# Tying the matmuls of the first pass to the written order of two layers, and gathering the token sums in half of each expert

## The chip, the cores and the metric

One core of a Trainium2 chip runs the whole program. The metric is the device time of one execution in microseconds (us), given as a median over several executions.

## The reference

The model is a causal attention whose output feeds a mixture of eight experts. Only the second half matters here:

```python
x = attention(q, k, v, s)            # 2304 tokens x 512
P = sinkhorn(exp(x @ w_gate))        # 2304 x 8, eight rounds of normalizing
out = 0
for e in range(8):                   # each expert: 512 -> 1024 -> 512
    h = maximum(x @ w1[e], 0)
    out += P[:, e:e+1] * (h @ w2[e])
```

All of it is float32. The kernel gets that precision from a matmul type with fewer mantissa bits by splitting each operand into a high and a low part and adding three products (high x high, high x low, low x high).

## The kernel before

Expert 0 is done beside the attention. The other seven experts are done in three passes of 768 tokens. A pass is 28 units (7 experts of 4 units); a unit is 256 of an expert's 1024 hidden columns.

**Layer 1** of a unit is a 2x2 block product with seven block products instead of eight (a scheme of the Strassen family). `SEQ` gives the order of these seven ops: 11, T3 (of the unit before), T1, T4 (of the unit before), 22, 21, T2. `step1` issues one op: six matmuls of 384 columns (line 959) into one of three PSUM buffers named `c` (Z, A and B of the unit). Between two ops that use the same buffer, ScalarE copies (`t`) or VectorE adds (`z`, line 253) read it, and `relu_split` turns the sum into the two parts of a hidden tile `h`: a ScalarE relu (line 923) and after it a VectorE instruction (line 924). The hidden tiles lie in 18 buffers, four to a unit. One link is closer than the others: op 21 takes the buffer that op T4 of the unit before leaves, once the relu and the VectorE instruction have read it, and only op 22 stands between them.

**Layer 2** of the first pass is plain. `step2p(idx, i, ui, ci)` issues one block: six matmuls of 512 columns (line 1077) into a PSUM buffer `zz`, for expert `idx`, half `i` of its tokens, unit `ui` and token chunk `ci`. An expert has 24 blocks: 12 with `i` = 0, then 12 with `i` = 1. The pass has 168 blocks, and 196 ops of layer 1.

**The first pass** begins with 26 ops of layer 1. Then `plain_item` writes layer 2 block by block, and before each block as many ops of layer 1 as `pace` (28 ops in 24 blocks) allows: one, and at every sixth block two (T4 and 22).

**What else runs beside it.** `prep_w2` splits the raw `w2` of a unit (tile `r`) into `w2p`: a ScalarE cast (line 110), a GpSimd subtraction (line 111). Then it asks SyncE for the raw `w2` two units on. `sum_w2` makes sums of `w2` for the later passes on VectorE (tile `sb`, lines 250 and 253 are the helpers that issue each add and subtraction) and stores them (`w2d`). `w1_ahead` makes sums of `w1` (tile `s`) on VectorE and splits `w1` (`wp`) on ScalarE and GpSimd. `x_sums`, the generator `side`, makes token sums for the third pass in 43 small pieces on VectorE (tiles `sx`, `sc`, `sh`) with loads and stores. `behind()` ties instructions behind the latest `relu_split` on their engine, as far as the written order had got.

**Who sets the order.** The text of the kernel gives each instruction its priority. A planner that simulates the engines then orders each engine's instructions: at each moment the instruction of highest priority whose inputs it takes to be ready. So the two layers need not run in the written order. `tc.issue_after(m)` forces an instruction behind `m` on the same engine, without a semaphore. On the chip each engine takes its instructions in the planner's order.

Of the kernel before, what the change touches and what calls it, by code (L numbers as in the profile page):

```python
# [8 lines left out]
F32 = mybir.dt.float32  # L9
F32R = mybir.dt.float32r  # L10
AF = mybir.ActivationFunctionType
ALU = mybir.AluOpType
AX = mybir.AxisListType

P = 128
B, H, S, D = 4, 8, 576, 64
NT, DM, E, F = B * S, H * D, 8, 1024
# [3 lines left out]
NFC = FU // P  # L21
UPE = F // FU
# [23 lines left out]
def fused_kernel(ctx: ExitStack, tc: tile.TileContext, qT, kT, v, s, w_gate, wu, out):  # L46
    nc = tc.nc
# [57 lines left out]
    acc = {}  # L105
    cur = {}

    def split(dst, lo, src):

        nc.scalar.copy(dst, src)  # L110
        nc.gpsimd.tensor_tensor(out=lo, in0=src, in1=dst.bitcast(F32), op=ALU.subtract)

    def split_piece(u, pc, raw):
        if pc % 2 == 0:
# [212 lines left out]
    def load_head(h):  # L327
# [23 lines left out]
        out=s_sb, in0=s_sb, scalar1=0.0, scalar2=8.0, op0=ALU.max, op1=ALU.mult  # L351
# [12 lines left out]
        out=mask,  # L364
# [299 lines left out]
    for ti in range(NS + 3):  # L664
        if ti < NS:
            g, i = slots[ti]
# [154 lines left out]
    LEAD1 = 5  # L821
# [3 lines left out]
    def load_w1(si):  # L825
        if si < len(steps1):
            n, o, _ = steps1[si]
            t = hp[1].tile([P, 2, 2, P], F32R, name="w1o", tag="w1o", bufs=LEAD1 + 1)
            w1s[n, o] = t
            nc.sync.dma_start(  # L830
                out=t.rearrange("p a k c -> p a (k c)").bitcast(F32),
                in_=w1d[unit(n)][:, WOPS.index(o)],
            )
# [76 lines left out]
        hops[n, o] = t  # L910
        return t

    mark = {}

    def behind():
        st = ExitStack()
        for m in mark.values():
            st.enter_context(tc.issue_after(m.ins))
        return st

# [18 lines left out]
    def step1(si):  # L939
        n, o, q = steps1[si]  # L940
        if si >= NS1P:
            load_w1(si + LEAD1)
        else:
            w1_ahead(n if SEQ[q or 0][1] == 0 else n + 1, q)
        w = w1s.pop((n, o))
        p = items[n // UPE][0]
        x = xo[XOF[o]]
        s_ = un.setdefault(n, {})
        if o == "11":
            s_["Z"] = ps1.tile([P, 512], F32, name="c", tag="c")[:, :TP]  # L950
        if o == "T1":
            s_["A"] = ps1.tile([P, 512], F32, name="c", tag="c")[:, :TP]
        if o == "21":
            s_["B"] = ps1.tile([P, 512], F32, name="c", tag="c")[:, :TP]
        ps = s_[{"11": "Z", "T2": "Z", "T3": "Z", "T4": "Z", "T1": "A", "22": "A", "21": "B"}[o]]
        fresh = o in ("11", "T1", "21")
        for k in range(2):
            for t, (wl, xl) in enumerate(((0, 0), (0, 1), (1, 0))):
                nc.tensor.matmul(  # L959
                    ps,  # L960
                    lhsT=w[:, wl, k],
                    rhs=x[:, xl, k],
                    start=(fresh and k == 0 and t == 0),
                    stop=(k == 1 and t == 2),
                    skip_group_check=True,
                )
        if o == "11":
            s_["t1"] = tmp("t", 4)
            nc.scalar.copy(s_["t1"], ps)
        elif o == "T1":  # L970
            s_["t5"] = tmp("t", 4)
            nc.scalar.copy(s_["t5"], ps)
        elif o == "22":
            s_["t53"] = tmp("t", 4)
            nc.scalar.copy(s_["t53"], ps)
        elif o == "21":
            s_["z11"] = tmp("z", 4)
            add(s_["z11"], ps, s_["t1"], nc.vector)
            relu_split(n, "11", s_["z11"])
        elif o == "T2":  # L980
            s_["z12"] = tmp("z", 4)
            add(s_["z12"], ps, s_["t53"], nc.vector)
            relu_split(n, "12", s_["z12"])
        elif o == "T3":
            s_["z22"] = tmp("z", 4)
            add(s_["z22"], ps, s_["t5"], nc.vector)
            relu_split(n, "22", s_["z22"])
        elif n < NUP:
            relu_split(n, "21", ps)
            un.pop(n)  # L990
        else:
            c21, s1, s3, s2, s4 = (
                hp[1].tile([P, TP], F32, name="s", tag="s", bufs=5) for _ in range(5)
            )
            nc.scalar.activation(c21, ps, AF.Relu)  # L995
            clip_op(s1, s_["z22"], c21, ALU.add)
            plain_split(n, "S1", s1, nc.gpsimd)
            clip_op(s2, s_["z11"], s1, ALU.subtract)
            plain_split(n, "S2", s2, nc.vector)
            clip_op(s3, s_["z11"], c21, ALU.subtract)  # L1000
            plain_split(n, "S3", s3, nc.gpsimd)
            clip_op(s4, s_["z12"], s2, ALU.add)
            plain_split(n, "S4", s4, nc.vector)
            un.pop(n)
        if n % (UPE * (E - 1)) == UPE * (E - 1) - 1 and p + 1 < NTP:
            load_x(p + 1, XOF[o])
# [8 lines left out]
                out=r2[m].rearrange("p f d -> p (f d)"), in_=wu[unit(m), :, 1024:2048]  # L1015
            )

    def prep_w2(m):

        if m >= NUP:  # L1020
            return
        r = r2.pop(m)
        for f in range(NFC):
            w = hp[2].tile([P, 2, DM], F32R, name="w2p", tag="w2p", bufs=8)
            split(w[:, 0], w[:, 1], r[:, f])
            w2p[m, f] = w
        r2[m, "raw"] = r
        load_r2(m + 2)

    def sum_w2(m):  # L1030

        if m >= NUP:
            return
        r = r2.pop((m, "raw"))
        e, ui = divmod(unit(m), UPE)
        t13 = hp[3].tile([P, 2, DH], F32, name="sb", tag="sb", bufs=3)
        t24 = hp[3].tile([P, 2, DH], F32, name="sb", tag="sb", bufs=3)
        sub(t13, r[:, :, DH:], r[:, 0, :].rearrange("p (j d) -> p j d", d=DH), nc.vector)
        sub(t24[:, 0], t13[:, 0], r[:, 1, DH:], nc.vector)
        add(t24[:, 1], t24[:, 0], r[:, 1, :DH], nc.vector)  # L1040
        for o, t in ((0, t13), (2, t24)):
            nc.sync.dma_start(
                out=w2d[e][o : o + 2, :, ui, :].rearrange("t p d -> p t d"), in_=t
            )
# [22 lines left out]
    def step2p(idx, i, ui, ci):  # L1067
        p, e = items[idx]
        m = idx * UPE + ui
        if ui == 0:  # L1070
            zb[ci] = ps2.tile([P, 512], F32, name="zz", tag="zz", bufs=3)
        if e == 1 and ui == 1:
            scale_acc(6 * p + 3 * i + ci)
        for f in range(NFC):
            h, w = hops[m, f"{i + 1}{f + 1}"], w2p[m, f]
            for t, (a, b_) in enumerate(((0, 0), (0, 1), (1, 0))):
                nc.tensor.matmul(  # L1077
                    zb[ci],
                    lhsT=h[:, a, ci * P : (ci + 1) * P],
                    rhs=w[:, b_],  # L1080
                    start=(ui == 0 and f == 0 and t == 0),
                    stop=(ui == UPE - 1 and f == NFC - 1 and t == 2),
                )
        if ui == UPE - 1:
            c = 6 * p + 3 * i + ci
            gated(c, e, accs[c], zb[ci])
            if e == E - 1:
                store_out(c)
# [95 lines left out]
    def run1(upto):  # L1184
        nonlocal si
        while si < min(upto, len(steps1)):
            step1(si)
            si += 1
# [9 lines left out]

    xbuf = lambda a: hp[3].tile([P, 4, 2, 128], F32, name="sx", tag="sx", bufs=2)
    side = x_sums(hp[3], 2, 128, nc.vector, xbuf, nc.scalar.copy)  # L1200
    nl2 = [0]
    last = E - 2
    pace = float(si)

    def plain_item(idx):
        nonlocal pace
        for i in range(2):
            for ui in range(UPE):
                ahead = (
                    UPE * idx + 3 if (i, ui) == (0, 0)  # L1210
                    else UPE * (idx + 1) + ui - 1 if i == 1 and ui
                    else None
                )
                if ahead is not None and ahead != NUP - 1:
                    prep_w2(ahead)
                for ci in range(3):
                    if ci == 2 and ahead is not None and ahead != NUP - 1:
                        with behind():
                            sum_w2(ahead)
                    if idx < last:  # L1220
                        pace += 28 / 24
                        run1(min(int(pace), NS1P))
                        nl2[0] += 1
                        if nl2[0] > 12 and nl2[0] % 5 in (2, 4):
                            with behind():
                                next(side, None)
                    step2p(idx, i, ui, ci)

    for idx in range(last):
        plain_item(idx)  # L1230
    run1(NS1P)
    prep_w2(NUP - 1)
    sum_w2(NUP - 1)
    for _ in side:
        pass
    p0bctx.close()
    p0ctx.close()
    hp[1] = ctx.enter_context(tc.tile_pool(name="p12", bufs=1, reuse_waits="tile"))
    for k in range(LEAD1):
        load_w1(NS1P + k)  # L1240
    plain_item(last)
    p0ctx2.close()
    hp[0] = ctx.enter_context(
        tc.tile_pool(name="h12", bufs=1, side="right", reuse_waits="tile")
# [60 lines left out]
```

## Time and profile before

| what | value |
|---|---|
| median of 3 runs | 1757.98 us (1755.74 to 1759.18) |
| the profiled execution | 1764.02 us, of which the span of instructions is 1762.2 us |
| TensorE matmul busy | 1694.1 us (96%) |
| VectorE, ScalarE, GpSimd busy | 71%, 47%, 49% |
| mean granted TensorE clock | 0.987 |
| first pass, from its first op to its last block | about 436 to 907 us of the span |

PE is TensorE's matmuls, PEld its weight loads, DVE is VectorE, ACT ScalarE, POOL GpSimd, SP SyncE, which issues the transfers. The busy times overlap, so none of them alone says what limits the kernel. Row times are microseconds from the start of the span.

### The profile page before, as it was taken

How to read it: one execution, taken by the hardware profiler on the slowest of the kernel's cores; microseconds unless marked ns; L12 is line 12 of the kernel's file. 1: busy time of each engine (PE TensorE's matmuls, PEld its weight loads, DVE VectorE, ACT ScalarE, POOL GpSimd, SP SyncE). 2: the span in 40 equal slices, each digit the busy share in tenths (PEclk: the TensorE clock that was granted, in tenths of full speed). 3: DMA queues.
4: the chain of work that ended last, by engine and by line, in shares of the span. 5: the costliest groups of instructions: out<-in, count | busy, mean ns of one | idle time of the engine just before them, and what ended most of it. 6: DMA issues, size and time to landing. Idle time of an engine off the chain costs nothing.

```text
span 1762.2 us, 31207 instructions
## 1 busy us (share of the span) xinstructions
PE 1694.1 (96%) x11109; PEld 1585.5 (90%) x11109; DVE 1242.6 (71%) x2352; ACT 831.2 (47%) x1817; POOL 856.8 (49%) x761
## 2 busy tenths in 40 slices
PE   5889999999999999999999999999999999999998
PEld 4678888889888888888889999999999999999998
DVE  6867667555666767666448877777777777777775
ACT  4876665733444343433335444444444544444442
POOL 5549647512554544444414444445445554444454
PEclk9899999999999999999999999999999999999999
DMA  6667656364667658557596655565687655655652
GB/s 173 189 187 227 204 162 203 98 256 168 206 233 264 210 203 278 178 204 265 196 307 192 193 183 182 179 186 180 184 306 226 206 184 187 184 182 176 189 180 84
DMA packets 204986, 352.09 MB, mean 200 GB/s; under 512 B 21088, under 2 KB 103008, under 8 KB 204800
## 3 DMA queue, kind: packets, MB, share of 16 engines
q1 hardware_dynamic: 204512, 349.52, 62.2%
q8 instruction: 88, 1.44, 0.3%
q10 hardware_dynamic: 320, 0.59, 0.1%
q14 instruction: 66, 0.54, 0.1%
HBM read 249.94 MB, written 94.81 MB: 196 GB/s over the span
## 4 chain that ended last, share of the span: by engine, by line
PE 76%; DVE 12%; DMA 5%; issue 3%; SPq 1%; ACT 1%; POOL 1%; DVEq 0%; POOLq 0%; ACTq 0%
PE c L959 28%; PE zz L1130 12%; PE zz L1077 11%; PE y L1130 8%; PE g L146 4%; PE g L175 4%; DVE s L935 3%; PE sc L454 3%; PE pv L556 2%; PE tr L526 2%; DVE h L250 2%; PE c L146 2%; PE c L175 2%; DVE z L253 1%; DVE a L1061 1%
## 5 line engine op out<-in xcount | busy, mean ns | idle before, releaser
L250 POOL TENSOR_TENSOR w2o<-r,w2o 128x512 fp32r<-128x512 f32 x196 | 279.7, 1448 | 381.8 <-ACT w2o L1111 336.3
L1130 PE MATMUL zz<-w2o,h 128*128 128x256 f32 x2016 | 280.6, 282 | 1.4 <-DMA w1o<-w1d 1.4
L959 PE MATMUL c<-xS,w1o 128*128 128x384 f32 x1344 | 277.8, 339 | 1.6 <-DVE z L253 1.5
L1130 PEld LDWEIGHTS zz<-w2o,h 128*128 128x128 f32 x2016 | 269.6, 188 | 1.9 <-ACT h L923 1.8
L1077 PE MATMUL zz<-w2p,h 128*128 128x512 f32 x1008 | 251.8, 396 | 0.4 <-ACT h L923 0.4
L935 DVE SCALAR_TENSOR_TENSOR s<-z,s 128x384 f32<-128x384 f32 x224 | 206.4, 959 | 48.6 <-ACT s L995 43.6
L923 ACT ACTIVATE h<-z 128x384 fp32r<-128x384 f32 x252 | 130.4, 525 | 220.4 <-DVE z L253 218.6
L924 DVE SCALAR_TENSOR_TENSOR h<-z,h 128x384 fp32r<-128x384 f32 x252 | 182.5, 732 | 72.1 <-ACT h L923 68.1
L959 PEld LDWEIGHTS c<-xS,w1o 128*128 128x128 f32 x1344 | 226.4, 188 | 5.1 <-DVE z L253 2.5
L1077 PEld LDWEIGHTS zz<-w2p,h 128*128 128x128 f32 x1008 | 190.4, 190 | 35.3 <-ACT h L923 0.7
L1130 PE MATMUL y<-w2o,h 128*128 128x256 f32 x1512 | 206.4, 283 | 3.6 <-DVE a L1061 2.9
L1130 PEld LDWEIGHTS y<-w2o,h 128*128 128x128 f32 x1512 | 196.6, 188 | 8.3 <-DVE a L1061 7.2
L959 PE MATMUL c<-x,w1o 128*128 128x384 f32 x1008 | 202.4, 336 | 0.0
L253 DVE TENSOR_TENSOR z<-c,t 128x384 f32<-128x384 f32 x252 | 135.2, 549 | 70.1 <-PE c L959 69.0
L250 POOL TENSOR_TENSOR h<-s,h 128x384 fp32r<-128x384 f32 x112 | 137.9, 1237 | 85.7 <-ACT h L931 84.8
L959 PEld LDWEIGHTS c<-x,w1o 128*128 128x128 f32 x1008 | 171.2, 188 | 0.1
L1061 DVE SCALAR_TENSOR_TENSOR a<-zz,prob,a 128x256 f32<-128x256 f32 (+1 forms) x210 | 110.7, 530 | 77.1 <-PE zz L1130 52.8
L931 ACT CAST h<-s 128x384 fp32r<-128x384 f32 x224 | 112.7, 513 | 93.6 <-DVE s L935 92.4
L959 PE MATMUL c<-xS,wp 128*128 128x384 f32 x672 | 137.6, 348 | 14.8 <-DVE z L253 14.2
L959 PEld LDWEIGHTS c<-xS,wp 128*128 128x128 f32 x672 | 124.2, 196 | 21.5 <-DVE z L253 15.4
L250 POOL TENSOR_TENSOR wp<-s,wp 128x512 fp32r<-128x512 f32 x56 | 78.5, 1402 | 118.0 <-ACT wp L859 85.0
L1111 ACT CAST w2o<-r 128x1024 fp32r<-128x1024 f32 x98 | 102.5, 1047 | 58.8 <-PE y L1130 48.8
(141 smaller groups left out, 2765.1 us busy)
## 6 DMA issues: line engine op xcount, KB each, us to landing
w1o<-w1d SPq DMA_DIRECT2D x392, 256.0 KB
w1d<-wp SPq DMA_DIRECT2D x84, 512.0 KB
r<-wu SPq DMA_DIRECT2D x70, 512.0 KB
r<-w2d SPq DMA_DIRECT2D x56, 512.0 KB
sa<-wu SPq DMA_DIRECT2D x28, 512.0 KB
w2d<-sb SPq DMA_DIRECT2D x56, 256.0 KB
wraw<-wu SPq DMA_DIRECT2D x22, 512.0 KB
rawq<-qT SPq DMA_DIRECT2D x64, 144.0 KB
```

Of the source, the lines that this page charges most:

```text
L146: nc.tensor.matmul(ps[:, :n], lhsT=w1[:, w, o : o + P], rhs=xcols(b, x, k, n0, n), start=(k == 0 and t == 0), stop=(k == KD - 1 and t == 2),)
L175: nc.tensor.matmul(ps, lhsT=h[:, cs], rhs=w2[:, w, f * DM : (f + 1) * DM], start=(f == 0 and t == 0), stop=(f == NFC - 1 and t == 2),)
L250: (eng or nc.gpsimd).tensor_tensor(out=out, in0=a, in1=b, op=ALU.subtract)
L253: (eng or nc.gpsimd).tensor_tensor(out=out, in0=a, in1=b, op=ALU.add)
L923: mark["a"] = nc.scalar.activation(t[:, 0], z, AF.Relu)
L924: mark["v"] = nc.vector.scalar_tensor_tensor(out=t[:, 1], in0=z, scalar=0.0, in1=t[:, 0].bitcast(F32), op0=ALU.max, op1=ALU.subtract,)
L931: nc.scalar.copy(t[:, 0], z)
L935: nc.vector.scalar_tensor_tensor(out=out, in0=z, scalar=0.0, in1=other, op0=ALU.max, op1=op)
L959: nc.tensor.matmul(ps, lhsT=w[:, wl, k], rhs=x[:, xl, k], start=(fresh and k == 0 and t == 0), stop=(k == 1 and t == 2), skip_group_check= ...
L1061: nc.vector.scalar_tensor_tensor(out=a, in0=ps, scalar=prob[:, c, e : e + 1], in1=a, op0=ALU.mult, op1=ALU.add)
L1077: nc.tensor.matmul(zb[ci], lhsT=h[:, a, ci * P : (ci + 1) * P], rhs=w[:, b_], start=(ui == 0 and f == 0 and t == 0), stop=(ui == UPE - 1 a ...
L1130: nc.tensor.matmul(ps, lhsT=h[:, a, ci * P : (ci + 1) * P], rhs=w[:, ui, b_], start=(fresh and ui == 0 and t == 0), stop=(ui == UPE - 1 an ...
```

## The change

The matmuls of `step1` and `step2p` are put under `behind(pe)`. `pe` holds the last matmul of the group written before, and it is set from the 13th block on, until the last block of the pass. So from there on TensorE runs ops and blocks exactly as written.

The pieces of `side` are no longer called at the second and fourth of every five blocks. They are called at `ci` = 1 and 2 of the blocks with `i` = 0 (the first half of an expert's blocks), again not before the 13th block.

The end of layer 1 is no longer a place of its own in the text. The loop runs over all seven experts, and after the last op of layer 1, which comes before the second block of the last expert, `switch()` drains `side`, closes the two buffer pools and asks for the first `w1` tiles of the second pass. `prep_w2` and `sum_w2` of the last unit come at the first blocks of the last expert. `split` and `prep_w2` get a parameter `eng` that no call uses, so they stay as they are.

```diff
-    mark = {}
-
-    def behind():
+    mark, pe, ordered = {}, {}, [False]
+
+    def behind(marks=mark):
         st = ExitStack()
-        for m in mark.values():
+        for m in marks.values():
             st.enter_context(tc.issue_after(m.ins))
         return st
...
-        for k in range(2):
-            for t, (wl, xl) in enumerate(((0, 0), (0, 1), (1, 0))):
-                nc.tensor.matmul(
+        with behind(pe):
+            for k in range(2):
+                for t, (wl, xl) in enumerate(((0, 0), (0, 1), (1, 0))):
+                    mm = nc.tensor.matmul(
...
+        if ordered[0]:
+            pe["m"] = mm
...
-        for f in range(NFC):
-            h, w = hops[m, f"{i + 1}{f + 1}"], w2p[m, f]
...
+        with behind(pe):
+            for f in range(NFC):
+                h, w = hops[m, f"{i + 1}{f + 1}"], w2p[m, f]
...
+        if ordered[0]:
+            pe["m"] = mm
...
-    nl2 = [0]
-    last = E - 2
+    nl2 = 0
     pace = float(si)
-
-    def plain_item(idx):
-        nonlocal pace
+    switched = False
+
+    def switch():
+        for _ in side:
+            pass
+        p0bctx.close()
+        p0ctx.close()
+        hp[1] = ctx.enter_context(tc.tile_pool(name="p12", bufs=1, reuse_waits="tile"))
+        for k in range(LEAD1):
+            load_w1(NS1P + k)
+
+    for idx in range(E - 1):
         for i in range(2):
             for ui in range(UPE):
                 ahead = (
                     UPE * idx + 3 if (i, ui) == (0, 0)
                     else UPE * (idx + 1) + ui - 1 if i == 1 and ui
-                    else None
+                    else NUP
                 )
-                if ahead is not None and ahead != NUP - 1:
-                    prep_w2(ahead)
+                prep_w2(ahead)
                 for ci in range(3):
-                    if ci == 2 and ahead is not None and ahead != NUP - 1:
+                    if ci == 2 and ahead < NUP:
                         with behind():
                             sum_w2(ahead)
-                    if idx < last:
+                    if si < NS1P:
                         pace += 28 / 24
                         run1(min(int(pace), NS1P))
-                        nl2[0] += 1
-                        if nl2[0] > 12 and nl2[0] % 5 in (2, 4):
+                        if i == 0 and nl2 > 12 and ci:
                             with behind():
                                 next(side, None)
+                    elif not switched:
+                        switched = True
+                        switch()
+                    nl2 += 1
+                    ordered[0] = nl2 > 12
                     step2p(idx, i, ui, ci)
-
-    for idx in range(last):
-        plain_item(idx)
-    run1(NS1P)
-    prep_w2(NUP - 1)
-    sum_w2(NUP - 1)
-    for _ in side:
-        pass
-    p0bctx.close()
-    p0ctx.close()
-    hp[1] = ctx.enter_context(tc.tile_pool(name="p12", bufs=1, reuse_waits="tile"))
-    for k in range(LEAD1):
-        load_w1(NS1P + k)
-    plain_item(last)
+    ordered[0] = False
     p0ctx2.close()
```

## Rows read from the trace of the kernel before

**Rows 1.** The page's head and its busy times over the whole span.

```profile
span 1762.2 us, 31207 instructions
...
PE 1694.1 (96%) x11109; PEld 1585.5 (90%) x11109; DVE 1242.6 (71%) x2352; ACT 831.2 (47%) x1817; POOL 856.8 (49%) x761
```

**Rows 2.** Stretches of the first pass: length, busy us of each engine, granted clock, DMA.

```profile
436.00:501.00 65.00, 61.78 (x313) 56.55 (x312) 45.02 (x64) 30.30 (x63) 34.92 (x27) 0.97 0.72 248
...
540.00:551.00 11.00, 8.44 (x47) 7.81 (x46) 10.41 (x21) 4.92 (x12) 3.98 (x3) 1.00 0.94 295
551.00:607.00 56.00, 56.00 (x280) 50.22 (x279) 37.02 (x61) 22.12 (x49) 27.35 (x21) 1.00 0.65 220
607.00:621.00 14.00, 11.46 (x51) 10.24 (x50) 11.04 (x18) 5.14 (x11) 5.19 (x4) 0.88 1.02 351
...
808.00:821.00 13.00, 10.49 (x47) 9.58 (x46) 10.58 (x18) 4.93 (x11) 5.04 (x5) 0.87 0.88 283
...
870.00:891.00 21.00, 16.36 (x68) 14.20 (x67) 9.91 (x20) 2.58 (x6) 0.34 (x1) 0.84 0.98 355
...
501.00:891.00 390.00, 372.64 (x1805) 333.67 (x1804) 250.88 (x411) 148.46 (x319) 173.19 (x135) 0.97 0.65 223
```

**Rows 3.** The same view of line 959 alone, layer 1 (PE, then PEld).

```profile
436.00:497.00 61.00, 42.64 (x219) 40.03 (x220) 0.97 0.71 244
...
436.00:612.00 176.00, 95.54 (x498) 89.04 (x498) 0.99 0.67 225
```

**Rows 4.** The same view of line 1077 alone, layer 2.

```profile
436.00:497.00 61.00, 18.87 (x72) 13.25 (x72) 0.97 0.71 244
...
436.00:612.00 176.00, 84.83 (x342) 63.61 (x342) 0.99 0.67 225
```

**Rows 5.** The chain that ended last, in order of time: start, us, what.

```profile
589.24 2.09 PE c L959 x12
591.33 4.58 PE zz L1077 x20
...
891.04 16.32 PE zz L1077 x72
```

**Rows 6.** Timeline of PE and DVE around 610 us: start, us; idle before, releaser.

```profile
613.16 3.59 PE L959 MATMUL c<-xS,wp 128*128 128x384 f32 x14 [2.54 <-DVE z L253]
...
607.97 1.78 DVE L250 TENSOR_TENSOR sb<-r 128x512 f32<-128x512 f32 x1
610.21 0.43 DVE L250 TENSOR_TENSOR sb<-sb,r 128x256 f32<-128x256 f32 x1 [0.45 <-DMA w2d<-sb]
610.56 1.75 DVE L250 TENSOR_TENSOR s<-sa 128x512 f32<-128x512 f32 x1
...
612.56 1.01 DVE L253 TENSOR_TENSOR z<-c,t 128x384 f32<-128x384 f32 x2
```

**Rows 7.** Timeline of SP and ACT around 665 us: a raw `w2` tile and its cast.

```profile
663.34 0.51 SPq L1014 DMA_DIRECT2D r<-wu  x1
...
669.49 1.14 ACT L110 CAST w2p<-r 128x512 fp32r<-128x512 f32 x2 [1.91 <-DMA r<-wu]
```

**Rows 8.** Who waited for whom, 501 to 891 us: us in total, times, longest.

```profile
ACT w2p L110 <- DMA r<-wu: 13.9, 6, 4.1
```

**Rows 9.** Timeline of DVE at the end of layer 1.

```profile
879.28 0.43 DVE L250 TENSOR_TENSOR sb<-sb,r 128x256 f32<-128x256 f32 x1 [3.30 <-DMA w2d<-sb]
...
880.68 1.01 DVE L253 TENSOR_TENSOR z<-c,t 128x384 f32<-128x384 f32 x2
```

**Rows 10.** Timeline of ACT, DVE and POOL: the two halves of `relu_split`, subtractions beside GpSimd.

```profile
541.13 0.49 ACT L923 ACTIVATE h<-c 128x384 fp32r<-128x384 f32 x1 [3.68 <-PE c L959]
...
541.65 0.56 DVE L924 SCALAR_TENSOR_TENSOR h<-c,h 128x384 fp32r<-128x384 f32 x1 [0.40 <-ACT h L923]
...
671.61 1.53 DVE L924 SCALAR_TENSOR_TENSOR h<-z,h 128x384 fp32r<-128x384 f32 x1 [2.96 <-ACT h L923]
...
678.12 0.68 DVE L250 TENSOR_TENSOR sb<-r 128x512 f32<-128x512 f32 x1
...
607.85 1.35 POOL L250 TENSOR_TENSOR wp<-s,wp 128x512 fp32r<-128x512 f32 x1 [2.26 <-ACT wp L859]
```

More of the change, by code (lines that the diff above doesn't have):

```diff
@@ L106, in fused_kernel, with split @@
     cur = {}
-    def split(dst, lo, src):
+    def split(dst, lo, src, eng=None):
         nc.scalar.copy(dst, src)
-        nc.gpsimd.tensor_tensor(out=lo, in0=src, in1=dst.bitcast(F32), op=ALU.subtract)
+        (eng or nc.gpsimd).tensor_tensor(
+            out=lo, in0=src, in1=dst.bitcast(F32), op=ALU.subtract
+        )
     def split_piece(u, pc, raw):
@@ L956, in step1 @@
         fresh = o in ("11", "T1", "21")
-        for k in range(2):
-            for t, (wl, xl) in enumerate(((0, 0), (0, 1), (1, 0))):
-                nc.tensor.matmul(
[L960 to L966, printed above, removed]
+        with behind(pe):
+            for k in range(2):
+                for t, (wl, xl) in enumerate(((0, 0), (0, 1), (1, 0))):
+                    mm = nc.tensor.matmul(
+                        ps,
+                        lhsT=w[:, wl, k],
+                        rhs=x[:, xl, k],
+                        start=(fresh and k == 0 and t == 0),
+                        stop=(k == 1 and t == 2),
+                        skip_group_check=True,
+                    )
+        if ordered[0]:
+            pe["m"] = mm
         if o == "11":
@@ L1016, in load_r2, with prep_w2 @@
             )
-    def prep_w2(m):
+    def prep_w2(m, eng=None):
         if m >= NUP:
@@ L1024, in prep_w2 @@
             w = hp[2].tile([P, 2, DM], F32R, name="w2p", tag="w2p", bufs=8)
-            split(w[:, 0], w[:, 1], r[:, f])
+            split(w[:, 0], w[:, 1], r[:, f], eng)
             w2p[m, f] = w
@@ L1073, in step2p @@
             scale_acc(6 * p + 3 * i + ci)
-        for f in range(NFC):
-            h, w = hops[m, f"{i + 1}{f + 1}"], w2p[m, f]
[L1076 to L1083, printed above, removed]
+        with behind(pe):
+            for f in range(NFC):
+                h, w = hops[m, f"{i + 1}{f + 1}"], w2p[m, f]
+                for t, (a, b_) in enumerate(((0, 0), (0, 1), (1, 0))):
+                    mm = nc.tensor.matmul(
+                        zb[ci],
+                        lhsT=h[:, a, ci * P : (ci + 1) * P],
+                        rhs=w[:, b_],
+                        start=(ui == 0 and f == 0 and t == 0),
+                        stop=(ui == UPE - 1 and f == NFC - 1 and t == 2),
+                    )
+        if ordered[0]:
+            pe["m"] = mm
         if ui == UPE - 1:
```

## The prediction, made before the changed kernel was run

> **What bounds the kernel now.** I read the page first: TensorE's matmuls are busy 96% of the span [rows 1], so a change of order can only give back idle time and time at a low clock. The change touches the first pass alone, so the view of stretches comes next. From 501 to 891 us the matmuls are busy 372.64 of 390 us [rows 2]: 17.36 us idle. That idle time is not spread: a long stretch such as 551 to 607 us has none. It comes once per expert. I cut the pass at the places where a slice was not full, and found six: five where one expert's blocks give way to the next (three of them shown, 540 to 551, 607 to 621 and 808 to 821 us) and one at the end of layer 1 (870 to 891 us) [rows 2].
>
> The last one has 21 - 16.36 = 4.64 us of idle, so the five have 17.36 - 4.64 = 12.72 us, about 2.5 us each. After most of them the granted clock is lower too: 0.88 of 14 us and 0.87 of 13 us, which is 1.7 us lost each time, and 0.84 of 21 us, 3.4 us, at the end; 1.00 after the first [rows 2]: after its wait TensorE runs for a few us at the lower of its two levels. Four of the five drop, and 0.97 over all 390 us agrees, so the five boundaries cost 12.7 + 4 x 1.7 = 19.5 us, and the end of layer 1 costs 4.6 + 3.4 = 8.0 us. Together 27.5 us: the most that order can give back after 501 us.
>
> **Why the boundaries stall.** The counts of matmuls by line say in which order TensorE ran. By 612 us it had 498 / 6 = 83 ops of layer 1 [rows 3] and 342 / 6 = 57 blocks of layer 2 [rows 4]. The text has written 26 + 57 x 28/24 = 92 ops by the 57th block. So layer 1 is 9 ops behind the text: the planner filled waits that it foresaw in layer 1 with blocks that were written later. Block 57 is the last unit's first block of its expert (2 x 24 + 9, counting from 0) and needs both first halves of unit 11's hidden tiles, which op 7 x 11 + 6 = 83 (counting from 0) completes. That op is just the next one. So the blocks have caught up with layer 1, and nothing is left to fill with. At that moment layer 1 itself waits: matmul 613.16 stood 2.54 us for an addition `z` [rows 6], and before that addition VectorE worked off a `w2` sum of 1.78 us, 0.45 us of waiting for a store of the sum before, and a `w1` sum of 1.75 us [rows 6].
>
> The `w2` sums are late for the same reason. They are tied behind the `relu_split` of the written order, which layer 1 reaches 9 ops late. A raw `w2` buffer is free only after its sum, so the load of the next waits too: one was issued at 663.34 us, and ScalarE stood 1.91 us for it before the cast [rows 7]. There are six such waits, 13.9 us in all, the longest 4.1 us [rows 8].
>
> **The change part by part.** The forecast is a sum against the profiled execution, 1764.0 us (span 1762.2), which is 6.0 us above the median of 1758.0.
>
> *Order of the matmuls.* No instruction and no semaphore is added. An op costs 2.09 / 2 = 1.05 us and a block 16.32 / 12 = 1.36 us [rows 5]. In the written order the blocks stay 9 to 11 ops behind what they need (26 + 57 x 28/24 = 92 against 83), some 22 us, so no block waits for a hidden tile. By counting allocations against finished blocks I get at most 14 to 16 hidden tiles alive, of 18, so the greater lead doesn't run out of buffers. Between two ops stands one block. An addition `z` has then 1.36 + 1.05 + 1.36 = 3.8 us until its buffer is wanted, and the sums come in the gaps, since each is tied behind a `relu_split` that now is done on time. I take the five boundary stalls as gone: **-19.5 us** (bounds 0 and -19.5).
>
> *The tight link.* At every sixth block the text puts T4 and 22 together, so op 21 comes 1.05 + 1.36 = 2.4 us after T4. The chain takes 1.1 us in the trace: T4's relu starts at 541.13, and the VectorE half ends at 541.65 + 0.56 = 542.21 [rows 10]. That leaves 1.3 us. A sum of 1.78 us just in front [rows 6] makes it 0.5 us late; if the VectorE half takes 1.53 us as well [rows 10], 1.78 + 1.53 + 0.54 - 2.4 = 1.45 us late. There are 22 such links after the 13th block: 0 to 32 us. VectorE is busy 64% of the stretch (250.88 of 390) [rows 2], about half of it with sums, so I take a third of the links at 0.5 us: **+3.4 us**.
>
> The row of 671.61 beside that of 541.65 [rows 10] shows that VectorE slows beside GpSimd, and so does a `w2` subtraction: 0.68 us at 678.12 alone, 1.78 us at 607.97, when GpSimd ran one of 1.35 us from 607.85 [rows 6, 10]. The Trainium skill (SBUF — State Buffer, section "SBUF: two separate sides") says that the two engines share a port pair as an exclusive lock, held for a whole instruction, where the VectorE operation has two SBUF inputs; these rows agree. By that rule a late link would wait for whole GpSimd instructions too, and the term would lie nearer to the 16 us of the second rival than to 3.4 us.
>
> *The catch-up.* At 497 us layer 1 has 219 / 6 = 36.5 ops [rows 3] with 72 / 6 = 12 blocks done [rows 4]; the text has 40. From the 13th block on these 3.5 ops must come first, with no block to fill. The stretch 436 to 501 us, mostly layer 1 alone, idles 3.2 us in 65 [rows 2]. Bounds 0 and 5 us; I take **+2 us**.
>
> *The end of layer 1.* There VectorE stood 3.30 us for a store of a `w2` sum, beside loads for the second pass (DMA 0.98 [rows 2]), with the additions `z` at 880.68 behind it [rows 9]. The loads are still asked for by the last unit's ops, and two of the last three `w2` sums still come among these ops, but the last one is now written after them, and 22 blocks remain after layer 1 instead of 12 (72 matmuls [rows 5]), so that what is late later is covered by 30 us of blocks. Bounds 0 and -8.0; I take half: **-4 us**.
>
> *Token sums.* The same 43 pieces, no byte more. They had about nine per expert evenly; now they have eight in the first half, where one `w2` sum falls, and none in the second, where three fall. Their cost is in the link's term; the loads for a piece are issued seven pieces ahead, as before. I take 0, covered by the 36% of VectorE that is free; without that cover it is in the link's upper bound. *Switch:* two blocks later in the text, under 22 blocks (30 us): 0. The stale tie that holds the second pass behind the last block costs 0: none of its ops ran earlier before.
>
> Sum: -19.5 + 3.4 + 2 - 4 = -18.1. From 1764.0 that is 1745.9, and from the median **1740 us**.
>
> **The rivals.** *Slower: ScalarE's wait now reaches TensorE.* Today a cast that stands for its `w2` load (up to 4.1 us [rows 8]) costs nothing, since blocks fill in. Tied, a relu behind it on ScalarE makes the next op late by 4.1 + 1.1 - 2.4 = 2.8 us, every later block waits with it, and the clock falls as after the stalls of today (1.7 us). Once per expert that is 6 x 4.5 = 27 us: 1740 + 27 = 1767 us. It decides from 3 us a time on. Against it: the load should come some 14 us (six pairs) before its cast once the sums are on time. The Trainium skill (PSUM — Partial Sum Buffer, section "Engine vs sequencer instructions") says that matmuls start and complete in program order, so a waiting one holds all behind it; 613.16 [rows 6], with no block slipping past, agrees.
>
> *The tight link eats the gain.* All 22 links late by the middle of 0 and 1.45, 0.72 us: 16 us instead of 3.4, so 1753 us. For it: VectorE is denser now in the first half of an expert, and there beside GpSimd's splits its rows are long [rows 10].
>
> *It does not do what it says.* If the `w2` and `w1` sums still meet in front of one `z` at each boundary, in whatever order TensorE runs, 1757 us. Against it: stretches without a boundary have no idle at all.
>
> **Chances.** Forecast 62% (own range 1731 to 1749: all 27.5 us back, or half the boundaries); tight link 17%; no effect 9%; slower 12%. What this measurement can tell from no change is about 0.2%, 3.5 us. Faster by more: 62% and most of the tight link, 75%; same 12%; slower 13%. Range 1730 to 1760: from all of 27.5 us back up to just past no effect.
>
> **What would show it.** PE's timeline alternates six and six matmuls from about 500 us on; no idle and a clock of 1.00 at the boundaries; far shorter waits of the cast for `r`; 132 matmuls of layer 2 after the last op; the pass ends near 889 us instead of 907. I am wrong if many small waits of PE on `z`, `h` or `t` appear, above all before op 21, or if waits of layer 1 behind ScalarE's casts do.

## The result and the profile after

The changed kernel takes 1739.7 us (median of 6 runs, 1738.24 to 1745.13) against 1757.8 us (6 runs, 1755.51 to 1761.94): a ratio of 0.990, 95% interval 0.988 to 0.992. The forecast was 1740. The profiled execution is 1738.24 us with a span of 1736.5, that is 25.8 us below the one of before. The pair of profiles shows more than the medians, because the profiled execution of before lay 6 us above its median and that of after 1.5 us below. TensorE, VectorE, ScalarE and GpSimd run as many instructions as before, by the counts of the busy times [rows 1].

The page's head (span; busy times) and the stretches (length, busy us of PE, PEld, DVE, ACT, POOL, granted clock, DMA) of the kernel after:

```profile
span 1736.5 us, 31221 instructions
...
PE 1682.0 (97%) x11109; PEld 1574.6 (91%) x11109; DVE 1238.2 (71%) x2352; ACT 838.3 (48%) x1817; POOL 855.8 (49%) x761
```

```profile
426.00:491.00 65.00, 61.31 (x313) 55.26 (x312) 41.70 (x60) 31.11 (x64) 33.42 (x26) 1.00 0.63 218
491.00:845.00 354.00, 351.67 (x1758) 316.52 (x1757) 245.79 (x411) 155.23 (x319) 173.22 (x137) 1.00 0.72 243
845.00:881.00 36.00, 36.00 (x165) 30.32 (x164) 12.19 (x15) 5.61 (x9) 6.25 (x5) 1.00 0.71 255
881.00:907.00 26.00, 24.09 (x144) 23.36 (x142) 13.12 (x22) 12.81 (x27) 3.56 (x3) 1.00 0.72 225
```

The second row answers to 501 to 891 us of before [rows 2]: idle time of TensorE has gone from 17.36 us to 354.00 - 351.67 = 2.33 us, and the granted clock from 0.97 to 1.00. All five boundary stalls are gone. What is left of idle there is nearly all one wait, at the end of layer 1. PE's timeline of the kernel after shows it, and the new order before it:

```profile
571.31 1.55 PE L1083 MATMUL zz<-w2p,h 128*128 128x512 f32 x6
572.69 1.21 PE L962 MATMUL c<-x,wp 128*128 128x384 f32 x6
573.74 1.55 PE L1083 MATMUL zz<-w2p,h 128*128 128x512 f32 x6
575.13 1.21 PE L962 MATMUL c<-xS,wp 128*128 128x384 f32 x6
576.17 1.20 PE L962 MATMUL c<-x,wp 128*128 128x384 f32 x6
577.21 1.55 PE L1083 MATMUL zz<-w2p,h 128*128 128x512 f32 x6
578.60 1.21 PE L962 MATMUL c<-xS,wp 128*128 128x384 f32 x6
...
588.33 1.21 PE L962 MATMUL c<-x,wp 128*128 128x384 f32 x6
589.38 1.20 PE L962 MATMUL c<-xS,wp 128*128 128x384 f32 x6
...
844.42 1.32 PE L962 MATMUL c<-xS,wp 128*128 128x384 f32 x6 [2.20 <-DVE z L255]
```

Six and six matmuls in turn; at 575.13 and at 588.33 two ops that stand together. The same view of stretches for each layer alone (line 962, then line 1083) gives the lag of layer 1. It starts at 425 us, because the pass of this kernel begins at 433.85 us, 2.5 us earlier than before:

```profile
425.00:612.00 187.00, 105.62 (x546) 96.40 (x546) 1.00 0.73 247
...
425.00:612.00 187.00, 86.61 (x335) 62.12 (x336) 1.00 0.73 247
```

By 612 us 546 / 6 = 91 ops and 335 / 6 = 56 blocks have run, and the text has 26 + 56 x 28/24 = 91: no lag is left. Before it was 83 ops with 57 blocks, 9 behind the text [rows 3, 4]. The waits of the `w2p` cast for its load, 13.9 us before [rows 8], no longer appear among the waits from 491 us on; one of 0.9 us stands ahead of that.

One thing got worse. Where the second pass begins, 881 to 907 us idles 26.00 - 24.09 = 1.91 us. The 26 us after the last block of the kernel before idle 0.60 us (its stretches):

```profile
908.00:934.00 26.00, 25.40 (x154) 24.99 (x153) 16.59 (x28) 16.33 (x34) 4.96 (x4) 1.00 0.83 256
```

ScalarE's timeline of the kernel after shows why: the scaling of an accumulator tile that is still on its way stands in front of a copy `t`, for which the op of layer 1 at 887.81 (line 962) waits 0.99 us. Five of the experiments with tied matmuls have such a wait for `t` there too, of 0.75 to 0.98 us.

```profile
886.67 0.72 ACT L1060 ACTIVATE a<-a,prob 128x512 f32<-128x512 f32 x1 [2.83 <-DMA a<-accd]
887.30 0.46 ACT L980 COPY t<-c 128x384 f32<-128x384 f32 x1
```

### The profile page after: what moved, and what is told of

It reads as the page before. It is cut to its first block, busy times and chain, and to the rows that moved or that the text cites. A ratio compares the mean times of both kernels' runs of the same rounds, so it can differ in the third digit from the quotient of the medians.

```text
span 1736.5 us, 31221 instructions
## 1 busy us (share of the span) xinstructions
PE 1682.0 (97%) x11109; PEld 1574.6 (91%) x11109; DVE 1238.2 (71%) x2352; ACT 838.3 (48%) x1817; POOL 855.8 (49%) x761
## 4 chain that ended last, share of the span: by engine, by line
PE 78%; DVE 11%; DMA 4%; issue 3%; POOL 2%; SPq 1%; ACT 1%; DVEq 0%; POOLq 0%; ACTq 0%
PE c L962 29%; PE zz L1083 13%; PE zz L1138 12%; PE y L1138 8%; PE g L148 3%; PE g L177 3%; DVE s L937 3%; PE sc L456 2%; PE pv L558 2%; DVE h L252 2%; PE tr L528 2%; PE c L148 2%; PE c L177 2%; DVE a L1066 1%; DVE z L255 1%
## 5 line engine op out<-in xcount | busy, mean ns | idle before, releaser
L1083 PE MATMUL zz<-w2p,h 128*128 128x512 f32 x1008 | 256.4, 393 | 0.5 <-ACT h L925 0.4
L962 PEld LDWEIGHTS c<-xS,wp 128*128 128x128 f32 x672 | 119.5, 188 | 13.5 <-DVE z L255 4.6
```

The costliest lines, as they stand in the source:

```text
L962: mm = nc.tensor.matmul(ps, lhsT=w[:, wl, k], rhs=x[:, xl, k], start=(fresh and k == 0 and t == 0), stop=(k == 1 and t == 2), skip_group_c ...
L1083: mm = nc.tensor.matmul(zb[ci], lhsT=h[:, a, ci * P : (ci + 1) * P], rhs=w[:, b_], start=(ui == 0 and f == 0 and t == 0), stop=(ui == UPE ...
```

## The experiments

All ratios are to the kernel before on the same chip; a value of about 0.990 is that of the full change. The kernel before took 1757.8 us beside the change and 1759.9 to 1760.4 us beside the experiments, so the ratios compare better than the medians.

**Order alone.** The loop and the tie of the change, the token sums as before:

```diff
-                        if i == 0 and nl2 > 12 and ci:
+                        if nl2 >= 12 and (nl2 + 1) % 5 in (2, 4):
```

> The matmuls are tied as in the change, the token sums stay at two of every five blocks. Theory (the order alone keeps layer 2 from catching up with layer 1, and the place of the token sums is worth nothing): within 4 us of the changed kernel's 1740 us, no stall of TensorE at an expert's boundary. Rival (the boundary stalls come from token sums and w2 sums that meet on VectorE, and gathering the token sums is what helped): 1752 us or more, with waits for z at the boundaries.

1742.9 us, ratio 0.9909 (0.9891 to 0.9928). The order alone gives nearly all. TensorE waits for `z` at 496.9, 533.3 and 581.7 us, 3.1 us together; the full change has none of these. So the place of the token sums is worth something in waits, though the medians do not tell the two apart.

**Token sums alone.** The change without the tie (the line `ordered[0] = nl2 > 12` left out).

> The token sums are gathered in the first half and the loop is the new one, but no matmul is tied. Theory: the boundary stalls stay, 1755 to 1760 us, and layer 1 lies some 9 ops behind the text at 612 us. Rival (the token sums are the cause): 1745 us or less.

1755.8 us, ratio 0.9973 (0.9955 to 0.9991). By 612 us 83 ops and 57 blocks have run, as in the kernel before. The stalls stay at five boundaries (0.88 to 2.65 us) and at the end of layer 1 (3.51 us); two of them in PE's timeline:

```profile
612.23 3.42 PE L962 MATMUL c<-xS,wp 128*128 128x384 f32 x18 [2.65 <-DVE z L255]
677.60 4.98 PE L962 MATMUL c<-xS,wp 128*128 128x384 f32 x18 [2.60 <-DVE z L255]
```

The gathering is worth a little by itself, some 5 us (0.27% of 1758), but it is not what ends the stalls.

**The loop alone.** Neither tie nor gathering, only the end of layer 1 written the new way.

> Only the new loop with the later end of layer 1: no tie, token sums as before. Theory: the five boundary stalls stay and at most the stall at the end of layer 1 shrinks, 1753 to 1760 us. Rival (the way the end of layer 1 is written gave most of the gain): 1745 us or less.

1757.9 us, ratio 0.9996 (0.9980 to 1.0013): nothing. The five stalls stay (2.17 to 3.05 us), and at the end of layer 1 TensorE still waits, 4.44 us against 4.64.

**Half a tie.** Blocks of layer 2 are tied behind the last op of layer 1 written before them; ops are not tied, and blocks leave no mark:

```diff
-        with behind(pe):
+        with behind({}):
             for k in range(2):
...
-        if ordered[0]:
-            pe["m"] = mm
         if ui == UPE - 1:
```

> Only blocks of layer 2 are tied, each behind the last op of layer 1 written before it; ops of layer 1 and the blocks among themselves are free. Theory (all that matters is that no block runs ahead of the ops written before it): within 4 us of 1740 us, no boundary stall. Rival (the strict turn of op and block matters, since it spaces the ops of layer 1 by a block each): ops of layer 1 bunch again, TensorE waits for z or h, 1748 us or more.

1739.3 us, ratio 0.9887 (0.9867 to 0.9907): as good as the full tie. Its stretch, in the same columns as above:

```profile
490.00:850.00 360.00, 359.08 (x1792) 322.58 (x1791) 266.16 (x418) 155.21 (x325) 183.77 (x140) 1.00 0.72 244
```

0.92 us idle in 360, and no wait at the end of layer 1. So it is enough that no block runs ahead of the ops written before it. The strict turn is not needed.

**Token sums in the second half.** As the change, but:

```diff
-                        if i == 0 and nl2 > 12 and ci:
+                        if i == 1 and nl2 > 12 and ci:
```

> As the change, but the token sums come in the second half of each expert, where three of its four w2 sums fall too. Theory (in the tied order a z has 3.8 us until its buffer is wanted, and the sums fit in the gaps): 1738 to 1747 us, single waits of 1 to 2 us. Rival (the place of the sums decides; only the first half has room): 1752 us or more, with a wait of TensorE in each second half.

1752.8 us, ratio 0.9962 (0.9949 to 0.9975). This went against me, and the rival's time was right, though not every second half has a wait: by the ratios some 11 of the 17 us are lost again, by the medians 13 of 18. Its largest waits are 4.09 us (796.01) and 3.45 us. VectorE's timeline ahead of the second, and PE's:

```profile
512.59 0.96 DVE L252 TENSOR_TENSOR sb<-sb,r 128x256 f32<-128x256 f32 x1
513.58 1.40 DVE L255 TENSOR_TENSOR sb<-sb,r 128x256 f32<-128x256 f32 x1
514.91 0.68 DVE L252 TENSOR_TENSOR s<-sa 128x512 f32<-128x512 f32 x1
515.51 0.55 DVE L255 TENSOR_TENSOR z<-c,t 128x384 f32<-128x384 f32 x1
...
517.53 1.49 DVE L252 TENSOR_TENSOR s<-s,sa 128x256 f32<-128x256 f32 x1
518.94 1.34 DVE L255 TENSOR_TENSOR sc<-sc,sx 128x128 f32<-128x128 f32 x1
520.21 0.55 DVE L255 TENSOR_TENSOR z<-c,t 128x384 f32<-128x384 f32 x1
```

```profile
513.72 1.21 PE L962 MATMUL c<-xS,wp 128*128 128x384 f32 x6
514.77 1.20 PE L962 MATMUL c<-x,wp 128*128 128x384 f32 x6
515.81 1.55 PE L1083 MATMUL zz<-w2p,h 128*128 128x512 f32 x6
520.81 2.29 PE L962 MATMUL c<-xS,wp 128*128 128x384 f32 x6 [3.45 <-DVE z L255]
```

Sums of `w2` (`sb`), `w1` (`s`) and tokens (`sc`) follow one another, and the `z` of the op at 513.72 comes at 520.21 only. The op at 520.81 needs its buffer and stands 3.45 us, with everything behind it. In a tied order the place of the sums matters.

**Half a tie, token sums in the second half.** The two edits together.

> Only blocks of layer 2 tied, behind the ops of layer 1 written before them, and the token sums in the second half of each expert. In the full tie that place of the token sums cost 13 us. If the cost comes from the strict turn (each op of layer 1 must wait its block, and a late z holds all): 1746 us or less here, since layer 1 may run ahead of its turn and build room. If it comes from VectorE alone, which works without a gap for some 10 us with the z at the end: 1749 to 1757 us here too.

1745.7 us, ratio 0.9917 (0.9894 to 0.9939), just inside the time that was to speak for the strict turn, and between 1739.3 and 1752.8. Three waits for `z` are left from 500 to 850 us beyond the one at its start (0.65), 5.8 us together, all after 660 us. That layer 1 builds room by running ahead of its turn is not shown: by 612 us it has run 88 ops with 53 blocks, which is what the text has, and at 660 us, ahead of the first of the three waits, 109 with 71, which is again the text's number. What saved the 7 us against the full tie stays open.

**A later load of the raw `w2`.** `load_r2(m + 1)` in place of `load_r2(m + 2)`, and one load instead of two at the start.

> As the change, but the raw w2 of a unit is asked for three blocks (7 us) before its cast instead of six (14 us). It tests the slower rival: a cast that stands for its load on ScalarE, with a relu behind it. Theory of the prediction (the tied order has 2.4 to 3.8 us of room, and a wait beyond that holds all of TensorE): loads take 5 to 6 us to land where the transfers are dense, so waits of the cast of 1 to 4 us return; where they pass 3 us TensorE stalls: 1742 to 1765 us. Against it (the tied order has cover enough for any such wait): within 4 us of 1740 us although the casts wait.

1740.3 us, ratio 0.9888 (0.9872 to 0.9903): no loss. From 495 us on no cast waits for its load (before that one block waits 1.03 us for a cast), so 7 us is early enough, and what such a wait would do to the tied order was not brought about.

**The order from the first block on.** `ordered[0] = True`.

> As the change, but the order is forced from the first block on, not from the 13th. Theory (layer 1 is behind the text by some four ops at the 13th block because its inputs come late at the start, so forcing the order there takes the filler away): 1740 to 1748 us, more idle of TensorE before 490 us. Rival (any tie helps): 1737 us or less.

1741.9 us (1735.32 to 1746.15), ratio 0.9896 (0.9877 to 0.9915): no difference from the change. Its idle from 420 to 490 us is 3.3 us, against 3.7.

**The `w2` sums untied.** The kernel before, with `sum_w2` called outside `behind()`.

> The kernel before, with the w2 sums no longer tied behind the latest relu_split; no tie of matmuls. It tests the prediction's step that the w2 sums and with them the w2 loads are late because they wait for a layer 1 that runs behind the text. If the late sums are what makes the boundary stalls: 1750 us or less and no waits of the cast for its load. If layer 2's catching up with layer 1 is enough by itself: the stalls stay, 1754 to 1762 us, although the casts no longer wait.

1756.1 us, ratio 0.9983 (0.9971 to 0.9994). No cast waits for its load any more and the time hardly moves, as the second of the two says. Still it does not settle the question, since two things happen. Its stretches:

```profile
420.00:490.00 70.00, 62.09 (x308) 56.91 (x307) 48.44 (x71) 30.17 (x61) 29.50 (x23) 0.93 0.69 235
490.00:850.00 360.00, 349.89 (x1725) 309.89 (x1724) 245.62 (x394) 145.99 (x311) 172.49 (x136) 1.00 0.66 222
```

At the boundaries the stalls split into smaller waits (10.1 us of idle in 490 to 850, against 12.7 before) and the clock stays up. But the start idles 7.9 us and the clock is 0.93 there. Layer 1 is further behind than before: counted from the start of the pass, 477 / 6 = 79.5 ops with 335 / 6 = 56 blocks at 612 us, where the text has 91.

**A longer link.** Between T4's relu and its VectorE half, subtractions that write what that half overwrites; two in the changed kernel, four in it, four in the kernel before:

```diff
         mark["a"] = nc.scalar.activation(t[:, 0], z, AF.Relu)
+        for _ in range(extra):
+            sub(t[:, 1], t[:, 0].bitcast(F32), t[:, 0].bitcast(F32), nc.vector)
```

> As the change, with two subtractions of 128x384 (some 0.5 us each) put into the tight link: between the relu of T4 and its VectorE half, writing what that half overwrites. 28 times 1.0 us more on VectorE, results unchanged. Theory (the link has 2.4 us and needs 1.1, so 1.3 us of room): 1739 to 1745 us. Rival (the link is already at its limit): 22 x 1 us more, 1760 us.

> The same with four subtractions, 2.0 us. Theory: 1.1 + 2.0 = 3.1 us against 2.4, each of 22 links 0.7 us late or more with a sum in front: 1752 to 1770 us, waits of TensorE before op 21. Rival (there is more room than the 2.4 us, or the planner places the subtractions elsewhere): under 1746 us.

> The kernel before, untied, with the same four subtractions. Theory (free order has blocks to fill the longer link, and pays only at the boundaries): within 6 us of the kernel before. Rival (the free order pays for it as the tied one does): 12 us or more over the kernel before.

1755.3 us (ratio 0.9964, 0.9948 to 0.9980), 1779.3 us (1.0104, 1.0083 to 1.0125) and 1797.2 us (1.0204, 1.0182 to 1.0227): three misses of the theories. First, a subtraction costs twice what I took; the group of two (busy, mean ns):

```profile
L252 DVE TENSOR_TENSOR h<-h 128x384 fp32r<-128x384 f32 x56 | 62.2, 1110 | 50.3 <-ACT h L925 49.4
```

So two lengthen the link by 2.2 us, not 1.0. Second, the link has more room than I said, and the next section says why. With two, the waits of TensorE for its VectorE half are nine, 4.3 us in all; what grows beside them are the waits for `z` (5.6 us) and the start. With four it is `z` that TensorE waits for, 11 times and 17.4 us, against 6.3 us for the link:

```profile
PE c L964 <- DVE z L255: 17.4, 11, 2.7
PE c L964 <- DVE h L928: 6.3, 2, 3.1
```

Nine of the eleven are of one kind, T3 of a unit that waits for the `z` of its T2:

```profile
527.32 1.21 PE L964 MATMUL c<-xS,wp 128*128 128x384 f32 x6
528.37 1.20 PE L964 MATMUL c<-x,wp 128*128 128x384 f32 x6
529.41 1.55 PE L1085 MATMUL zz<-w2p,h 128*128 128x512 f32 x6
532.98 1.31 PE L964 MATMUL c<-xS,wp 128*128 128x384 f32 x6 [2.02 <-DVE z L255]
```

The two waits for the link stand before op 11, at 682.56 and 748.54, not before op 21: at 675.78 an op 21 ran 6 us ahead of the VectorE half (681.96) whose buffer I thought it takes. So this run does not measure the link from T4 to 21.

Third, the untied order pays as well: its stretch and, under it, that of the tied kernel with four.

```profile
490.00:850.00 360.00, 330.49 (x1583) 292.37 (x1582) 280.82 (x460) 136.37 (x288) 163.59 (x123) 0.97 0.63 213
```

```profile
490.00:850.00 360.00, 339.89 (x1662) 302.13 (x1661) 302.01 (x485) 148.73 (x307) 172.58 (x130) 0.99 0.69 227
```

29.5 us of idle against 20.1, at a clock of 0.97 against 0.99. Without the subtractions the same 360 us idle 12.7 and 2.3 us, so the four add 16.8 us of idle to the untied order and 17.8 to the tied one. The ratios rise by 0.020 in both. The free order covers a late VectorE no better than the tied one, and no worse.

## Why the prediction was right, and where it was not

**The boundary stalls (-19.5 us): right, and shown.** 12.72 us of idle and the clock's falls are gone, under the tie alone (order alone 0.9909, token sums alone 0.9973, loop alone 0.9996). Half a tie shows what in it works: blocks may not run ahead of the ops written before them. The lag of 9 ops fell to none. Two of the five stalls were of another kind than I described: at 678.25 and at 811.81 (2.50 us) an op of layer 1 waited for T4's VectorE half and not for `z`. The tie ended them as well.

```profile
678.25 3.15 PE L959 MATMUL c<-x,wp 128*128 128x384 f32 x12 [2.87 <-DVE h L924]
```

**Why they stalled: half shown.** That the stalls need blocks that run ahead of the text is shown by the half tie. I added that the late `w2` sums make the loads late and so feed the stall. The casts' waits do vanish with the tie, but freeing the sums alone, which ends these waits too, gave 0.2% and made the start worse. The late loads are a companion of the lag and not shown to be a cause of the stalls.

**The numbering of the ops: wrong, without effect on the sum.** The first unit has five ops, not seven, since no unit stands before it whose T3 and T4 could come along. So every op's number is two less than I gave. T2 of unit 11 is number 81 and had run by 612 us; block 57 then waited for its addition `z` on VectorE and the relu behind it, which is where the row of the `z` pair points [rows 6]. And the two ops written together are not T4 and 22; the description of the kernel above has the same mistake. The pair at 575.13 in the kernel after reads `xS` and then `x`: it is T2 and 11, and ScalarE's timeline has the copy of op 11 (line 974) right behind it:

```profile
578.28 0.53 ACT L925 ACTIVATE h<-z 128x384 fp32r<-128x384 f32 x1 [2.18 <-DVE z L255]
578.72 0.46 ACT L974 COPY t<-c 128x384 f32<-128x384 f32 x1
```

The first row says also that the `z` of T2 was done at about 578.3, 0.3 us before T3 at 578.60 needed it.

The pair does not stay the same. `pace` adds 28/24 as a rounded number, and the rounding decides whether an op comes a block earlier or later. From the 13th block on T2 and 11 stand together six times (up to 575.13), then 21 and T2 eleven times (`x` and then `xS`, 588.33 to 745.78), then T2 and 11 again five times (762.80 to 826.42), and at the end T2 and T3 (841.01).

**The tight link (+3.4 us): the wrong link, and mis-sized.** T4 to 21 has two blocks and an op between, 3.8 us, not 2.4. The link with 2.4 us is T2 to T3 where T2 and 11 stand together, through the addition `z`, 0.55 us without a queue. That leaves 1.8 us. There are 11 such places, not 22, since a pair of 21 and T2 leaves two blocks and an op between T2 and T3 too. In the changed kernel none of them is late between 491 and 840 us: 0 us in place of 3.4. The experiments show where it turns. With four subtractions eight of the nine waits of T3 come behind a pair of T2 and 11, the ninth at the end of layer 1, and none behind the eleven pairs of 21 and T2 (613.22 to 778.03). With the token sums in the second half it is the same, as at 520.81: 9.9 us of waits are of T3 behind such a pair or at the end, and one of 0.86 us is elsewhere.

I also took 1.53 us for T4's VectorE half from the row at 671.61 [rows 10]. That row reads `z` and `h`; T4's half reads the PSUM buffer `c` and `h`, as the row at 541.65 does. By form (busy, mean ns) in the kernel before:

```profile
L924 DVE SCALAR_TENSOR_TENSOR h<-z,h 128x384 fp32r<-128x384 f32 x84 | 74.7, 899 | 37.0 <-ACT h L923 34.6
L253 DVE TENSOR_TENSOR z<-c,t 128x384 f32<-128x384 f32 x84 | 44.1, 551 | 55.5 <-PE c L959 55.4
L924 DVE SCALAR_TENSOR_TENSOR h<-c,h 128x384 fp32r<-128x384 f32 x28 | 15.6, 556 | 46.9 <-ACT h L923 46.7
```

The two forms that read `c` keep their 0.55 us; only the one with both inputs outside PSUM is slowed at times, to 1.53 us or more. So the instructions of the links themselves are not what gets long. What makes them late is what stands in front of them.

**The token sums (0): wrong as a rule, right for this place.** I put the link's worst case at one `w2` sum in front of a `z`. In the second half three kinds of sums come one after another, and a `z` starts 6.5 us after its op did (513.72 to 520.21). The places rank: first half 1739.7, evenly 1742.9 (its interval includes the first), second half 1752.8. The last is the size of the second rival, the gain eaten by a late VectorE, which the place chosen avoids.

The rule of the Trainium skill that I set beside it (SBUF — State Buffer, section "SBUF: two separate sides": VectorE with two SBUF inputs and GpSimd hold a port pair in turn) is agreed to by the sums of one size that take 0.68 or 1.78 us [rows 6, 10], by the subtractions' mean of 1.11 us, and by the three forms just shown. The changed kernel shows no loss from it in the pass; the experiments with more work on VectorE do not separate it from the work itself.

**The catch-up (+2 us): not seen.** The start idles 3.7 us (65.00 - 61.31) where it idled 3.2, and the clock is 1.00 there instead of 0.97, one fall of 1.7 us less. Forcing the order from the first block on changes nothing that can be measured.

**The end of layer 1 (-4 us): mis-sized, and given a wrong reason.** 4.64 us of idle became 2.20, and the clock no longer falls: -5.8 us. I put the gain down to the later last `w2` sum and the blocks behind it. But the loop alone has both and still waits 4.44 us there, so it was the tie that shortened the wait. Behind the last op 138 matmuls ran (23 blocks), not 132, and the pass ended at about 879 us, not 889. What is left has another cause than I named: the last T3 stands right behind the last T2, as no op 11 follows, and the wait is for T2's `z`, one tile after another in VectorE's queue.

**The second pass (0): wrong by 1.3 us,** by the accumulator's scaling on ScalarE, which no step of mine looked at.

**The sum: luck in part.** From its first op to the first of the second pass, with the same 2185 matmuls, the pass took (before, then after):

```profile
436.33:907.20 470.87, 450.29 (x2185) 403.36 (x2184) 298.33 (x477) 181.14 (x384) 213.14 (x166) 0.97 0.67 230
433.85:879.33 445.48, 439.46 (x2185) 393.65 (x2184) 295.24 (x477) 189.44 (x387) 212.88 (x166) 1.00 0.72 243
```

That is 25.4 us less. The steps in it are 12.7 us of idle at the boundaries, four falls of the clock (6.8), the end of layer 1 (5.8) and the start (1.7 - 0.5), together 26.5; the 1.1 us between I can't place. The pass also began 2.5 us earlier, where nothing of the change has run yet, and behind it 2.2 us were lost, 1.3 of them at the start of the second pass. The median moved by 18.1 us only; the executions of before lie between 1753.9 and 1768.4 us. The sum of -18.1 was worked out from the profiled execution, whose pass gave back 25.4 us; for that one it was too small. It was then taken from the median, and no profile shows how much the median execution had to give back. That the forecast came within a microsecond of the median is therefore luck; the mechanism of its largest term is not.

**The slower rival** did not come about. Its premise, the cast that stands for its load, went away with the lag, and a load half as early did not bring it back. What a late ScalarE would do to the tied order is therefore not shown. A late VectorE, at least, costs the tied order as much as the untied one (0.020 of the ratio each).

## What to carry to other kernels

Count what each of two interleaved layers has done at a moment, and compare it with the text: here a planner that fills foreseen waits spent the lead of one layer over the other, and when it was spent both waited for the same late result. A tie that only kept the consumer from running ahead of the text was enough, and added no instruction to TensorE or to the three engines that serve it. In a tied order look next at what stands in the helper engine's queue in front of each result that TensorE needs, and put optional work where that queue is short. Look also at where two ops stand together: here a rounding decided it, and only the pairs of one kind left a link so short that a longer queue showed.

## What was not expected of the hardware

The granted clock did not follow the length of a wait alone. In the kernel before it stayed at 1.00 around a wait of 2.56 us and fell to 0.88 around one of 2.54 us [rows 2, 6]. Near 480 us both kernels have a wait of 1.76 us for `z` in front of 22 matmuls (before, then after):

```profile
481.62 5.66 PE L959 MATMUL c<-xS,wp 128*128 128x384 f32 x22 [1.76 <-DVE z L253]
479.06 4.09 PE L962 MATMUL c<-xS,wp 128*128 128x384 f32 x22 [1.76 <-DVE z L255]
```

Before, they take 1.6 us longer and the clock of the stretch is 0.97; after, it is 1.00. So part of what the medians and the profiles differ by may hang on whether a wait brings a fall.
